# Attention and a SwiGLU block on one core: sums moved to VectorE, weight sums stored later into more places

## The chip, the cores and the metric

The kernel runs on one core of a Trainium2 chip. A core has five engines that each work through a list of instructions of their own, in order, and wait for each other by semaphores: TensorE (PE in the profile, its weight loads PEld), VectorE (DVE), ScalarE (ACT), GpSimd (POOL) and SyncE (SP), which here only issues transfers between the chip's memory (DRAM) and the core's memory (SBUF). Matrix products land in PSUM, eight banks of 128 x 512 floats. The metric is the time of the whole program on the device, in microseconds.

## The reference

```python
def _attn_ref(q, k, v, g_q, g_k):          # (8, 12, 448, 64) each: sequences, heads, tokens, width
    def rmsnorm(x, g):
        return x / np.sqrt(np.mean(x * x, axis=-1, keepdims=True) + 1e-06) * g
    q_n, k_n = rmsnorm(q, g_q), rmsnorm(k, g_k)
    scores = np.matmul(q_n, k_n.transpose(0, 1, 3, 2)) / np.sqrt(64)
    attn = softmax(scores)                 # written out in the original
    return np.matmul(attn, v)

def _moe_ref(x, w_gate, w_val, w_out, rms_g):   # x: (8 * 448, 768); weights 768 x 1536, 768 x 1536, 1536 x 768
    xn = x / np.sqrt(np.mean(x * x, axis=-1, keepdims=True) + 1e-06) * rms_g
    g = xn @ w_gate
    silu = g * (1.0 / (1.0 + np.exp(-g)))
    return silu * (xn @ w_val) @ w_out
```

The second function gets the first one's output, with the twelve heads side by side.

## The kernel before, in words

`safe_scores` does the work (a slower twin, `any_scores`, stands behind a flag and does not run here). Sequence by sequence and pair of heads by pair of heads it does attention; the block behind it (gate, value and out projections) of sequence b runs in the gaps of the attention of sequence b+1. The order is written out by hand. Each call of `pe` is one **step**: it raises a clock `now["t"]`, emits its work, and then emits what is due; `after(n, fn)` makes `fn` due n steps later. All five engines receive their instructions in the order in which they are emitted. `fill` takes the next entries of a list `todo` (each a product of the gate and value stage, or a part of the out projection) as steps; between them stand the steps of attention.

The first sequence (b = 0) multiplies directly, while the weights are converted from 64-bit floats. From the second on (b = 1 to 7), fewer products and more sums are used. For gate and value there are four **groups** of columns in the order 0, 2, 1, 3, and in each group fifteen products (`PRODUCTS`: q3, q6, q8, q9, q4, q5, q7, q2, q0, q1, q14, q11, q12, q10, q13), each of a left factor (a block of the normed attention output or a sum of such blocks) and a right factor. Right factors are nine blocks of weights (`RAWS`, b11 to b33) and nine sums of two or three of them (`RIGHT_G`, v1 to v14). `three` emits a group. It accumulates products one on top of another in PSUM banks called B, X, Y and Z, and takes **snapshots** in between: the bank's content after a product is copied or added into one of the six result tiles c11 to c23, or into the helpers s and d, before the next product is put on top of it. Three other products lie between two uses of a bank (two lie between a product's snapshot and the next writing). `copy` is a copy by ACT (L1177), `plus` adds PSUM to an SBUF tile on DVE (L1180), `more` adds two SBUF tiles on GpSimd (L1183). `hand` turns a finished pair of result tiles into the gated hidden values.

The nine sums of weights of each group are made once, during the second sequence, by `derive` (L1072, L1075, on DVE), stored to DRAM by SP (L1078, `after(1, ...)`), and loaded again for every later sequence. `ask` emits loads of weights (L1052) in a fixed order (`uses`) as places come free. **Places** are pieces of an SBUF tile `arena`: 66 units of 128 columns, a block of gate and value weights takes four neighbouring units, a block of out weights three. While the sums for the out projection are made, 18 units are set aside ("side"); 48 remain, 12 places of four. `ask` goes on only while `keep_free` more places are free than the one it takes: 2 for the second sequence's gate and value weights. A block's place is given back when its last use has been emitted, and counts as free one step later. `derive` takes the sum that is next on its list if its sources were asked for at least five steps ago; if a product is up whose sum has not been emitted, `fill` emits the sum right before it.

The out projection is built the same way, with seven right factors for each half: B11, B21, T2, T3, T1, B22, T4, where the T's are sums. `derive_o` makes those (L1102), in six columns c of four sums each, in the places set aside; the loads of any T wait until all 24 sums are stored. For b = 2, 3, 5, 6 and 7 the out projection goes a level deeper (`out_quads`, L1496; its sums of weights are made by `derive_q`, L1130 to L1133), for b = 1 and 4 it doesn't (`out_strassen`, L1425). Its left factors are sums of hidden values: `left_sums` (L1344) makes S1 to S4 for a pair of row tiles, `left_q1` (L1370) the deeper level's.

Two attention instructions matter beside this: `turn` transposes q and k on PE, and ACT (L549) and DVE (L550, L552) take the result; at a sequence's end `rms_x` (L725) sums the squares of its output, which GpSimd has added up in `ss` (L643).

Of the kernel before, what the change touches and what calls it, by code (L numbers as in the profile page):

```python
# [25 lines left out]
BW = 384  # L26
# [309 lines left out]
def safe_scores(  # L336
# [498 lines left out]
    freed = [0] * (NW * BW // 128)  # L835

    def h_of(fc):
        return hs[fc // KG][:, fc % KG, :]
# [10 lines left out]

    def places(kind):  # L850

        lim = len(freed) - (zone() if count["done"] else 0)
        if kind == "wg":
            spans = [range(i, i + 4) for i in range(0, lim - 3, 4)]
        elif kind == "side":
            spans = [range(i, i + 3) for i in range(lim, len(freed), 3)]
        else:
            spans = [range(i - 3, i) for i in range(lim, 2, -3)]
        return [span for span in spans if None not in [freed[i] for i in span]]

    def block(kind="w"):
        span = min(places(kind), key=lambda span: (max(freed[i] for i in span), span[0]))
        for i in span:
            freed[i] = None
        return arena[:, span[0] * 128:span[-1] * 128 + 128], span

    def room(many, kind="w"):
# [2 lines left out]
    def give_back(key):  # L870

        span = st.pop(key)[1]

        def free():
            for i in span:
                freed[i] = now["t"]

        after(1, free)

    def data(key):  # L880
        return st[key][0]
# [65 lines left out]
    def convert():  # L947

        n = turn_of["n"]
        if n >= TURNS or not room(1):  # L950
            return False
        turn_of["n"] += 1
        if 0 <= n - 5 < len(pieces):
            key = pieces[n - 5][0]
            st[key] = block()
            lo, top = st.pop(("cv", n - 5))
            nc.gpsimd.tensor_tensor(data(key).bitcast(I32), top, lo, ALU.add)
        if 0 <= n - 4 < len(pieces):
            st["cv", n - 4] = join(*st.pop(("cv", n - 4)))
        if 0 <= n - 3 < len(pieces):  # L960
            st["cv", n - 3] = split(st.pop(("raw", n - 3)), n - 3)
        if n < len(pieces):
            st["raw", n] = load_raw(pieces[n][1])
        if 0 <= n - 7 < len(pieces):
            keep(pieces[n - 7][0])
        if turn_of["n"] == TURNS:
            count["done"] = True
            ends = [cv_tile(i, F32) for i in range(6)]
            whole = [raw_pool.tile([128, 2 * BW], F32, name="raw") for _ in range(7)]
            room_so.extend(whole[:6])  # L970
            more_x.extend((ends[4], ends[5], whole[6][:, 0:S]))
            homes = [t[:, 0:BW] for t in ends[:4]]
            carried.extend(t.rearrange("p (c n) -> p c n", c=KG) for t in homes)
        return True
# [51 lines left out]
    def ask():  # L1026

        if turn_of["n"] < TURNS:
            return
        while side and room(1, "side"):  # L1030
            key = side.pop(0)
            asked[key] = now["t"]
            st[key] = block("side")
            nc.sync.dma_start(out=data(key), in_=home(key))
        while asked["n"] < len(uses):
            key = uses[asked["n"]]
            kind, keep_free = "wg" if key[0] == "wg" else "w", 3
            if key[1] == 1 and key[0] == "wg":
                keep_free = 2
            elif asked["derived"] < len(derived):  # L1040
                return
            if key[0] == "wo" and key[2][0] == "T" and asked.get("sums_o", 0) < 4 * NFP:
                return
            if key[0] == "wq" and asked.get("sums_q", 0) < KG * (key[2] + 1):
                return
            if not room(keep_free + 1, kind):
                return
            asked["n"] += 1
            asked[key] = now["t"]
            st[key] = block(kind)  # L1050
            src = home(key)
            nc.sync.dma_start(out=data(key)[:, 0:src.shape[-1]], in_=src)  # L1052

    def derive(wait=5):

        if asked["derived"] >= len(derived):
            return False
        g, to = derived[asked["derived"]]
        first, minus, plus = RIGHT_G[to]
        sources = [part.lstrip("-") for part in (first, minus, plus) if part]  # L1060
        for name in sources:
            if ("wg", 1, g, name) not in st or asked.get(("wg", 1, g, name), 0) > now["t"] - wait:
                return False
        if not room(1, "wg"):
            return False
        asked["derived"] += 1
        key = ("wg", 1, g, to)
        st[key] = block("wg")
        parts = {name: data(("wg", 1, g, name)) for name in sources}
        at, t = parts[first], data(key)  # L1070
        if minus:
            nc.vector.tensor_tensor(t, at, parts[minus], ALU.subtract)  # L1072
            at = t
        if plus:
            nc.vector.tensor_tensor(t, at, parts[plus.lstrip("-")], ALU.subtract if plus[0] == "-" else ALU.add)  # L1075
        for name in sources:
            done_with(("wg", 1, g, name))
        after(1, lambda: nc.sync.dma_start(out=home(key), in_=t))  # L1078
        return True

    def done_with(key):

# [4 lines left out]
    sums_o = [(c, step) for c in range(NFP) for step in (("T1", "B12", "B11", "B11"), ("T3", "B22", "B12", "B12"),  # L1087
                                                          ("T2", "B22", "T1", "B22"), ("T4", "B21", "T2", "B21"))]

    def derive_o(wait=5):  # L1090

        if not sums_o:
            return
        c, (to, plus, minus, place) = sums_o[0]
        for name in BLOCKS:
            if asked.get(("wd", 1, name, c), now["t"]) > now["t"] - wait:
                return
        sums_o.pop(0)
# [3 lines left out]
        nc.vector.tensor_tensor(data(key), a, b, ALU.subtract)  # L1102

        def store():
            keep(key)
            asked["sums_o"] = asked.get("sums_o", 0) + 1

        after(1, store)
        if to == "T4":
            for name in ("T1", "T2", "T3", "T4"):  # L1110
                after(3, lambda name=name: used(("wd", 1, name, c)))
# [55 lines left out]
    def three(b, n):  # L1167
# [11 lines left out]
        def plus(name, ps):  # L1179
            nc.vector.tensor_tensor(T[name], ps[:, 0:S], T[name], ALU.add)  # L1180

        def more(name, one, other, what):
            nc.gpsimd.tensor_tensor(T[name], T[one], T[other], what)  # L1183

        def hand(name, j, wait):

# [44 lines left out]
        def q5(make):  # L1231
            T["pc"] = pair("pc")
            T["c13"], T["c23"] = T["pc"][:, 0], T["pc"][:, 1]
            copy("c13", make(bank["Y"]))
            more("c13", "c13", "s", ALU.add)
            more("c13", "c13", "d", ALU.subtract)

        def q7(make):
            copy("c23", make(bank["B"]))
            more("d", "c23", "d", ALU.subtract)  # L1240

        def q2(make):
            copy("c11", make(bank["X"]))
            more("c11", "c11", "d", ALU.add)

        def q0(make):
            copy("c23", make(bank["Y"]))
            more("c23", "c23", "s", ALU.add)

        def q1(make):  # L1250
            plus("c21", make(bank["B"]))

        def q14(make):
            plus("c12", make(bank["X"]))
# [13 lines left out]
            plus("c13", ps)  # L1268

        def q13(make):  # L1270
            if n == len(GROUPS) - 1 and in_quads(b):
                after(1, lambda: left_q1(b, 0, range(3)))
            plus("c13", make(bank["Z"]))
            after(1, lambda: hand("pc", 2, 1))
            if n % 2:
                after(3, lambda: sums(0))
                after(3 if n == len(GROUPS) - 1 else 5, lambda: sums(1))

        def sums(i):

            st["left_sums"] = now["t"]
            if i < len(out_pairs(b)):
                left_sums(b, i, n // 2)

        def run(fn, left, right):
            fn(lambda onto=None: product(b, g, left, right, onto))
# [50 lines left out]
    def left_sums(b, n, half):  # L1337

        pair, row = (0, n) if in_quads(b) else (n, 0)
        if half == 0:  # L1340
            for i, name in enumerate(("S1", "S2", "S4")):
# [2 lines left out]
        ops = [lambda args=args: nc.vector.tensor_tensor(*(of(name) for name in args[:3]), args[3])  # L1344
               for args in (("S1", "A21", "A22", ALU.add), ("S2", "S1", "A11", ALU.subtract),
                            ("S3", "A11", "A21", ALU.subtract), ("S4", "A12", "S2", ALU.subtract))]
        if half and in_quads(b):
            first_sums.extend(ops)
        else:
# [255 lines left out]
    def fill(n=None):  # L1605
# [8 lines left out]
        for _ in range(min(n, len(todo))):  # L1614
# [266 lines left out]
```

## Time and profile before

| what | value |
|---|---|
| median of three runs | 1613.95 us (1613.63 to 1617.66) |
| profiled execution, device time | 1614.22 us |
| its span, first to last instruction | 1612.4 us |
| PE busy / DVE / ACT / POOL | 1508.5 / 981.7 / 639.6 / 898.2 us |
| moved by DMA | 322.5 MB, 200 GB/s on average |
| granted TensorE clock, mean | 0.98 |

Rows of the profile name the line, the engine, the operation and the tile written and read (`w<-w` is a weight place computed from other places, `kept` and `kept_o` the DRAM copies). "ff" is any PSUM bank of the block, "l" the tiles of s, d and some left factors, "pa", "pb" and "pc" the pairs c12/c22, c11/c21 and c13/c23, "raw", "top" and "xs" left factors in tiles used earlier for something else. A row of a wait gives the waiter, the one waited for, total us, the number of times, and the longest. A row of the order of time gives the start, the length, the instructions merged into it, and in square brackets the idle time before it and what ended it. One product of the gate and value stage is eight rows of PE (x8).

### The profile page before, as it was taken

Reading aid. Unit: us, or ns where it says so; the run is one execution under the profiler, and the core shown is the slowest. Engines: PE = TensorE matmul, PEld = TensorE weight load, DVE = VectorE, ACT = ScalarE, POOL = GpSimd, SP = SyncE. Lnnn points to the kernel's source line nnn. Section 1 sums busy time; section 2 is a strip of 40 time slices with the busy share of each in tenths; the row PEclk is TensorE's granted clock in tenths of the full one; section 3 lists DMA queues with packets and bytes.
Section 4 is the critical chain, followed back from the end, with each engine's and each line's share of the span. In section 5 each row is a group of like instructions: output and inputs, shape, how many; then the busy total and the mean of one; then the engine's idle time right before and its main releaser. Section 6 shows DMA issues by size and latency. Waiting matters only on the chain. (4 is left out here: it accounts for less than half of the span.)

```text
span 1612.4 us, 25793 instructions
## 1 busy us (share of the span) xinstructions
PE 1508.5 (94%) x8732; PEld 1170.4 (73%) x8732; DVE 981.7 (61%) x1766; ACT 639.6 (40%) x1409; POOL 898.2 (56%) x848
## 2 busy tenths in 40 slices
PE   8999989887788898899999999999999999999997
PEld 4344445676654687778887888857887888899997
DVE  5788897776664277685455844344546834484454
ACT  6766653433422243333543335524553244202210
POOL 6877976664442276445766566566655654413212
PEclk9999999999988999999999999999999999999999
DMA  7767674664447789987545874567545774578666
GB/s 209 206 187 212 195 219 153 210 211 140 145 144 228 236 280 298 291 257 247 168 133 157 260 233 142 162 188 217 158 131 178 228 221 119 146 241 280 170 207 194
DMA packets 302176, 322.51 MB, mean 200 GB/s; under 512 B 81620, under 2 KB 243668, under 8 KB 302036
## 3 DMA queue, kind: packets, MB, share of 16 engines
q1 hardware_dynamic: 301108, 320.58, 64.9%
q8 instruction: 72, 1.18, 0.3%
q14 instruction: 68, 0.56, 0.1%
q10 hardware_dynamic: 800, 0.20, 0.1%
q0 software_dynamic: 128, 0.00, 0.0%
HBM read 266.90 MB, written 53.77 MB: 199 GB/s over the span
## 5 line engine op out<-in xcount | busy, mean ns | idle before, releaser
L1162 PE MATMUL ff<-x,w 128*128 128x224 f32 x1344 | 278.6, 362 | 20.5 <-DVE w L1075 12.4
L1162 PEld LDWEIGHTS ff<-x,w 128*128 128x128 f32 x1344 | 258.1, 195 | 28.9 <-issue 10.2
L713 POOL TENSOR_TENSOR es<-es,e 128x448 f32<-128x448 f32 x205 | 244.5, 1193 | 12.2
L1183 POOL TENSOR_TENSOR pc<-pc,l 128x448 f32<-128x448 f32 x84 | 98.7, 1175 | 254.2 <-ACT pc L1177 231.2
L658 PE MATMUL sc<-qT,kT 64*64 64x448 f32 x1176 | 232.0, 539 | 4.4 <-DVE kT L552 2.1
L673 PE MATMUL av<-e,vt 64*64 64x448 f32 x984 | 193.6, 538 | 0.0
L1162 PE MATMUL ff<-xs,w 128*128 128x224 f32 x896 | 181.5, 358 | 8.8 <-DMA w<-kept 4.7
L1162 PEld LDWEIGHTS ff<-xs,w 128*128 128x128 f32 x896 | 170.6, 194 | 13.9 <-issue 7.7
L663 ACT ACTIVATE e<-sc 128x448 f32<-128x448 f32 x294 | 155.2, 546 | 61.3 <-PE sc L658 45.8
L1180 DVE TENSOR_TENSOR pb<-ff,pb 128x448 f32<-128x448 f32 x56 | 34.8, 621 | 189.7 <-PE ff L1162 187.0
L658 PEld LDWEIGHTS sc<-qT,kT 64*64 64x64 f32 x1176 | 78.9, 133 | 88.7 <-issue 59.1
L1496 PE MATMUL ff<-w,l 128*128 128x192 f32 x630 | 119.0, 330 | 14.7 <-issue 8.7
L1496 PEld LDWEIGHTS ff<-w,l 128*128 128x128 f32 x630 | 103.4, 190 | 22.0 <-issue 12.1
L515 POOL TENSOR_TENSOR rs<-ms,mhalf 128x12 f32<-128x12 f32 (+1 forms) x50 | 116.6, 2332 | 4.2
L708 POOL TENSOR_TENSOR es<-e 128x448 f32<-128x448 f32 x41 | 47.3, 1153 | 124.4 <-ACT e L663 124.4
L1564 PE MATMUL ff<-x,w 128*128 128x448 f32 x288 | 112.8, 545 | 0.0
L1162 PE MATMUL ff<-top_x,w 128*128 128x224 f32 x448 | 93.0, 357 | 3.1 <-DVE w L1075 2.0
L673 PEld LDWEIGHTS av<-e,vt 64*64 64x64 f32 x984 | 66.4, 133 | 39.3 <-issue 39.3
L1162 PEld LDWEIGHTS ff<-top_x,w 128*128 128x128 f32 x448 | 83.1, 190 | 15.2 <-issue 12.3
L1564 PEld LDWEIGHTS ff<-x,w 128*128 128x128 f32 x288 | 53.8, 192 | 51.6 <-issue 49.6
L550 DVE COPY kT<-tr 128x64 f32<-128x64 f32 x48 | 10.6, 220 | 130.9 <-ACT qT L549 130.8
L1162 PE MATMUL ff<-l,w 128*128 128x224 f32 x448 | 89.7, 353 | 0.0
(188 smaller groups left out, 2902.8 us busy)
## 6 DMA issues: line engine op xcount, KB each, us to landing
w<-kept SPq DMA_DIRECT2D x396, 256.0 KB, 3.7
w<-kept_q SPq DMA_DIRECT2D x350, 192.0 KB, 3.7
w<-kept_o SPq DMA_DIRECT2D x150, 192.0 KB, 3.8
kept_q<-w SPq DMA_DIRECT2D x63, 192.0 KB, 3.7
qk<-in_q_dram SPq DMA_DIRECT2D x48, 192.0 KB, 3.5
qk<-in_k_dram SPq DMA_DIRECT2D x96, 96.0 KB, 3.5
raw<-in_moe_w_gate_dram SPq DMA_DIRECT2D x24, 384.0 KB, 4.7
raw<-in_moe_w_val_dram SPq DMA_DIRECT2D x24, 384.0 KB, 4.1
```

The lines of the kernel that those rows point to most:

```text
L515: nc.gpsimd.tensor_tensor(st["rs", g][:, cols], ms, mhalf[:, cols], ALU.pow)
L550: nc.vector.tensor_copy(st["kT", g][:, LAST], ps[:, S:])
L658: nc.tensor.matmul(ps[r, 0:S], lhsT=st["kT", g][r, keys_of(i)], rhs=st["qT", g][r, :], start=True, stop=True)
L663: nc.scalar.activation(e, ps[:, 0:S], ACT.Exp)
L673: nc.tensor.matmul(st["av", g][own(j), 0:S], lhsT=vt, rhs=st["e", g, i][r], start=i == 0, stop=i == PARTS - 1, skip_group_check=True)
L708: nc.gpsimd.tensor_tensor(st["es", g], st["e", g, 0], st["e", g, 1], ALU.add)
L713: nc.gpsimd.tensor_tensor(st["es", g], st["es", g], st["e", g, i], ALU.add)
L1162: nc.tensor.matmul(bank[:, w * HT:(w + 1) * HT], lhsT=data(key)[:, (2 * w + c) * 128:(2 * w + c + 1) * 128], rhs=a[left][:, c, :], start=o ...
L1180: nc.vector.tensor_tensor(T[name], ps[:, 0:S], T[name], ALU.add)
L1183: nc.gpsimd.tensor_tensor(T[name], T[one], T[other], what)
L1496: nc.tensor.matmul(ps, lhsT=a[:, j, :], rhs=data(key)[:, n % 2 * HW:(n % 2 + 1) * HW], start=start and j == 0, stop=j == KG - 1, skip_grou ...
L1564: nc.tensor.matmul(bank[w][:, 0:S], lhsT=data(key)[:, c * 128:(c + 1) * 128], rhs=st["x", 0][:, 3 * half + c, :], start=half == c == 0, st ...
```

## The change

- In `three`, five steps of a group change their snapshots. `copy` followed by `more` on GpSimd becomes one sum from PSUM on DVE (`onto`, or `plus`): c13 = bank + s (q5), c23 = bank + s (q0), c11 = bank - d (q7) and then bank + c11 (q2). c13 minus d becomes a sum of two SBUF tiles on DVE. d keeps its value; the new c11 takes over what d was used for.
- `derive` stores a sum five steps after it is made, not one, and the sum's place is given back only when its product and its store have both been emitted. Places of the second sequence's gate and value weights count as free three steps after being given back, not one.
- Six more places for that sequence: the first 512 columns of the six tiles `room_so`, in which the left sums of out projections lie later. Loads must leave six places free instead of two.
- In `fill`, `derive` may emit up to two or three instructions' worth of sums a step instead of one sum, and is called in two more steps early in a block; `derive_o` is called up to three times. T blocks are asked for once their own sum's store is emitted, which happens two steps after the sum, and a sum needs its sources asked for four steps ago instead of five.
- Since `room_so` is taken until the end of the second sequence's products, that sequence's sixteen left sums come after its last group, one in each step, instead of eight in the middle and eight at the end.
- In sequences with the deeper out projection, the first three left factors (`left_q1(b, 0, range(3))`) are emitted at q1 of the last group, not one step after q13.

```diff
+    spare = {}
...
         if kind[0:2] == "wg":
             spans = [range(i, i + 4) for i in range(0, lim - 3, 4)]
+            if kind == "wg1":
+                spans += [range(i, i + 4) for i in sorted(spare) if i % 4 == 0]
...
-        after(1, free)
+        after(3 if key[0:2] == ("wg", 1) else 1, free)
...
+            for i, t in enumerate(room_so):
+                spare[1000 + 4 * i] = t[:, 0:4 * 128]
+                freed.update({1000 + 4 * i + j: 0 for j in range(4)})
...
             if key[1] == 1 and key[0] == "wg":
-                keep_free = 2
+                kind, keep_free = "wg1", 6
...
-            if key[0] == "wo" and key[2][0] == "T" and asked.get("sums_o", 0) < 4 * NFP:
+            if key[0] == "wo" and key[2][0] == "T" and ("kept", *key[2:]) not in asked:
                 return
...
-        after(1, lambda: nc.sync.dma_start(out=home(key), in_=t))
-        return True
+        def store():
+            nc.sync.dma_start(out=home(key), in_=t)
+            done_with(key)
+
+        after(5, store)
+        return len(sources) - 1
...
-    def derive_o(wait=5):
+    def derive_o(wait=4):
...
-            asked["sums_o"] = asked.get("sums_o", 0) + 1
-
-        after(1, store)
+            asked["kept", to, c] = True
+
+        after(2, store)
...
     def used(key):
         give_back(key)
-        after(1, ask)
+        after(3 if key[0:2] == ("wg", 1) else 1, ask)
...
-        def more(name, one, other, what):
-            nc.gpsimd.tensor_tensor(T[name], T[one], T[other], what)
+        def onto(name, ps, other, what=ALU.add):
+            nc.vector.tensor_tensor(T[name], ps[:, 0:S], T[other], what)
...
-            copy("c13", make(bank["Y"]))
-            more("c13", "c13", "s", ALU.add)
-            more("c13", "c13", "d", ALU.subtract)
+            onto("c13", make(bank["Y"]), "s")
+            nc.vector.tensor_tensor(T["c13"], T["c13"], T["d"], ALU.subtract)
 
         def q7(make):
-            copy("c23", make(bank["B"]))
-            more("d", "c23", "d", ALU.subtract)
+            onto("c11", make(bank["B"]), "d", ALU.subtract)
 
         def q2(make):
-            copy("c11", make(bank["X"]))
-            more("c11", "c11", "d", ALU.add)
+            plus("c11", make(bank["X"]))
 
         def q0(make):
-            copy("c23", make(bank["Y"]))
-            more("c23", "c23", "s", ALU.add)
+            onto("c23", make(bank["Y"]), "s")
 
         def q1(make):
             plus("c21", make(bank["B"]))
+            if n == len(GROUPS) - 1 and in_quads(b):
+                left_q1(b, 0, range(3))
...
         def q13(make):
-            if n == len(GROUPS) - 1 and in_quads(b):
-                after(1, lambda: left_q1(b, 0, range(3)))
             plus("c13", make(bank["Z"]))
...
-            if i < len(out_pairs(b)):
+            if b == 1:
+                if n == len(GROUPS) - 1 and i == 0:
+                    jobs = [left_sums(b, pair, half) for pair in range(2) for half in range(2)]
+                    first_sums.extend(fns[k] for ks in ((0, 1), (2,), (3,)) for fns in jobs for k in ks)
+            elif i < len(out_pairs(b)):
                 left_sums(b, i, n // 2)
...
+            if 2 < now["t"] - st["block"] < 5:
+                derive()
             if now["t"] - st["block"] > 4 and now["t"] != st.get("left_sums"):
-                if not derive():
+                made = 0
+                while made < 2:
+                    done = derive()
+                    if not done:
+                        break
+                    made += done
+                for _ in range(3 - made):
                     derive_o()
-                derive_o()
                 derive_q()
```

More of the change, by code (lines that the diff above doesn't have):

```diff
@@ L834, in safe_scores @@
     arena = slots.tile([128, NW * BW], F32, name="w")
-    freed = [0] * (NW * BW // 128)
+    UNITS = NW * BW // 128
+    freed = {i: 0 for i in range(UNITS)}
+    spare = {}
     def h_of(fc):
@@ L850, in places @@
     def places(kind):
-        lim = len(freed) - (zone() if count["done"] else 0)
-        if kind == "wg":
+        lim = UNITS - (zone() if count["done"] else 0)
+        if kind[0:2] == "wg":
             spans = [range(i, i + 4) for i in range(0, lim - 3, 4)]
+            if kind == "wg1":
+                spans += [range(i, i + 4) for i in sorted(spare) if i % 4 == 0]
         elif kind == "side":
-            spans = [range(i, i + 3) for i in range(lim, len(freed), 3)]
+            spans = [range(i, i + 3) for i in range(lim, UNITS, 3)]
         else:
@@ L864, in block @@
             freed[i] = None
+        if span[0] in spare:
+            return spare[span[0]], span
         return arena[:, span[0] * 128:span[-1] * 128 + 128], span
@@ L1063, in derive @@
                 return False
-        if not room(1, "wg"):
-            return False
+        if not room(1, "wg1"):
+            return 0
         asked["derived"] += 1
         key = ("wg", 1, g, to)
-        st[key] = block("wg")
+        st[key] = block("wg1")
+        refs[key] = 2
         parts = {name: data(("wg", 1, g, name)) for name in sources}
@@ L1281, in sums @@
             st["left_sums"] = now["t"]
-            if i < len(out_pairs(b)):
+            if b == 1:
[3 more added lines that the diff above has]
+            elif i < len(out_pairs(b)):
                 left_sums(b, i, n // 2)
         def run(fn, left, right):
-            fn(lambda onto=None: product(b, g, left, right, onto))
+            fn(lambda ps=None: product(b, g, left, right, ps))
         by_name = dict(q0=q0, q1=q1, q2=q2, q3=q3, q4=q4, q5=q5, q6=q6, q7=q7, q8=q8, q9=q9, q10=q10, q11=q11, q12=q12, q13=q13, q14=q14)
@@ L1346, in left_sums @@
                             ("S3", "A11", "A21", ALU.subtract), ("S4", "A12", "S2", ALU.subtract))]
+        if b == 1:
+            return ops
         if half and in_quads(b):
```

## The prediction

> **What bounds the kernel now.** I read the page's first two parts, then the busy time of each engine in a few stretches, then who waited for whom on PE, then the same on the DMA queue of SP, then the order of time around the long waits.
>
> ```profile
> span 1612.4 us, 25793 instructions
> PE 1508.5 (94%) x8732; PEld 1170.4 (73%) x8732; DVE 981.7 (61%) x1766; ACT 639.6 (40%) x1409; POOL 898.2 (56%) x848
> ```
>
> PE is the bound: it is idle for 1612.4 - 1508.5 = 103.9 us, and only that, with what a lowered clock costs, can be won. In the stretches below the columns are the length, then the busy time of PE, PEld, DVE, ACT and POOL, the granted clock, the DMA share and GB/s.
>
> ```profile
> 100.00:200.00 100.00, 97.91 (x456) 48.16 (x455) 85.29 (x138) 66.79 (x153) 85.80 (x80) 1.00 0.66 191
> ...
> 300.00:320.00 20.00, 16.62 (x111) 12.62 (x115) 19.43 (x25) 6.07 (x12) 13.68 (x11) 1.00 0.58 204
> ...
> 300.00:460.00 160.00, 130.57 (x739) 107.97 (x739) 119.70 (x178) 56.40 (x122) 91.00 (x79) 0.90 0.51 167
> 460.00:560.00 100.00, 86.05 (x398) 49.24 (x399) 37.53 (x78) 24.86 (x55) 25.63 (x25) 0.93 0.68 212
> ...
> 560.00:1612.00 1052.00, 1007.86 (x6234) 874.46 (x6232) 593.89 (x1110) 375.16 (x826) 553.82 (x515) 0.99 0.66 205
> ```
>
> The stretch 300 to 460 (gate and value products of the second sequence, whose weight sums are made on the chip) holds 29.4 us of PE's idle time at a clock of 0.90; the next (that sequence's out projection) 14 at 0.93; the last 1052 us hold 44 at 0.99. PE's waits (total us, times, longest):
>
> ```profile
> PE ff L1162 <- DVE w L1075: 26.2, 11, 6.7
> PE ff L1425 <- DMA w<-kept_o: 9.4, 3, 8.5
> PE ff L1496 <- issue: 8.7, 5, 2.0
> PE msx L725 <- POOL ss L643: 7.7, 5, 1.9
> PE ff L1162 <- DVE pb L1180: 7.5, 6, 1.5
> PE ff L1162 <- DMA w<-kept: 4.7, 1, 4.7
> PE ff L1162 <- DVE w L1072: 2.8, 2, 1.6
> ```
>
> PE stands 26.2 + 2.8 = 29.0 us for sums of weights. DVE is not full there (119.70 of 160), so the sums are late because their sources are. SP's queue between 300 and 460 says why:
>
> ```profile
> SPq L1078 <- DVE w L1075: 48.6, 24, 8.8
> SPq L1078 <- DVE w L1072: 12.3, 4, 4.8
> SPq L1052 <- DVE w L1072: 12.0, 3, 9.0
> ```
>
> L1078 stores a sum, L1052 loads weights. SP issues in order, so for 48.6 + 12.3 = 60.9 us it stands at stores whose sum DVE has not made, with the next loads behind; for 12.0 us it stands at loads into a place that a sum still reads. The waits also cost clock:
>
> ```profile
> 313.39 1.75 PE L1162 MATMUL ff<-x,w 128*128 128x224 f32 x8 [0.60 <-DVE w L1075]
> ...
> 330.65 3.35 PE L1162 MATMUL ff<-raw,w 128*128 128x224 f32 x8 [3.83 <-DVE w L1075]
> ...
> 372.20 3.36 PE L1162 MATMUL ff<-raw,w 128*128 128x224 f32 x8 [6.73 <-DVE w L1075]
> ...
> 406.59 7.37 PE L1162 MATMUL ff<-x,w 128*128 128x224 f32 x24 [4.12 <-DVE w L1075]
> ...
> 443.31 3.33 PE L1162 MATMUL ff<-x,w 128*128 128x224 f32 x8 [3.22 <-DVE w L1075]
> ...
> 491.58 10.77 PE L1425 MATMUL ff<-w,raw 128*128 128x384 f32 x24 [8.51 <-DMA w<-kept_o]
> ...
> 518.45 8.01 PE L1425 MATMUL ff<-w,raw 128*128 128x384 f32 x24
> ```
>
> After a wait of 0.60 us a product takes 1.75 us, after one of over 3 us 3.33 to 3.36: 1.6 us lost each time, 2.1 in the group of 24 (7.37 against three times 1.75), 2.8 at 491.58 against 518.45. These four losses in the stage make 6.9 us; a mean clock of 0.90 over 160 us bounds the loss at 16.
>
> **The change, part by part.**
>
> *Snapshots.* 28 groups of products (four for each of seven sequences). Rows of the copy, of the sum on GpSimd, of a sum from PSUM on VectorE, and of the sums of weights (ns: least, median, most):
>
> ```profile
> L1177 ACT COPY pc<-ff x84: 512/532/534, 307.9 to 1543.5; 128x448 f32<-128x448 f32 x84
> L1183 POOL TENSOR_TENSOR pc<-pc,l x84: 1125/1132/1594, 308.5 to 1544.3; 128x448 f32<-128x448 f32 x84
> L1180 DVE TENSOR_TENSOR pc<-ff,pc x84: 607/615/626, 326.9 to 1553.4; 128x448 f32<-128x448 f32 x84
> L1072 DVE TENSOR_TENSOR w<-w x28: 674/682/1622, 300.0 to 456.0; 128x512 f32<-128x512 f32 x28
> L1075 DVE TENSOR_TENSOR w<-w x32: 677/692/1542, 301.6 to 456.8; 128x512 f32<-128x512 f32 x32
> ```
>
> Each group loses four copies (112 x 0.532 = 60 us of ACT) and five sums on GpSimd (140 x 1.13 = 158 us of POOL); DVE gets four sums from PSUM and one (c13 minus d) between SBUF tiles: 140 x 0.62 = 87 us, making 1068 of 1612. The one between SBUF tiles I price at 0.62 too; it could be stretched as the sums of weights are (1622 against 682), by 0.9 us at most. In the second sequence's stage DVE gets 20 x 0.62 = 12.4 us. A removed sum on GpSimd also stretches DVE less. The two kinds of weight sums took 25.29 and 30.84 us in the stage, against 28 x 0.682 + 32 x 0.692 = 41.2 unstretched: 14.9 us of stretching.
>
> ```profile
> 300.00:460.00 160.00, 25.29 (x28) 0.90 0.51 167
> ...
> 300.00:460.00 160.00, 30.84 (x32) 0.90 0.51 167
> ```
>
> POOL ran 79 instructions there, 20 of them go, so by share 20/79 x 14.9 = 3.8 us of it goes. The Trainium skill, "SBUF — State Buffer", section "SBUF: two separate sides", has a stronger rule: a VectorE instruction with two SBUF inputs and a GpSimd instruction lock each other out for a whole instruction. By that rule up to 20 x 1.13 = 22.6 us of stretching could go, bounded by the 14.9 that there is; the sum of the stage would then be some 11 us lower. The row of the sums from PSUM (607 to 626 ns in all 84) agrees that these are not locked out.
>
> *Stores five steps later, places freed three steps later, six more places, two sums a step.* A step is one entry in the hand-made order; a product is one of 1.75 us. Five steps on, the sum has been made when SP meets its store, and the place after three steps no longer has a reader. Nothing is added to SP: the same 36 stores. What a later store costs is its place, held longer. Places were 12 (48 units of 4), and a load was asked for with 3 of them free; now there are 18 and 7 must be free: 11 instead of 9 can be taken when a load goes out, and seven stay for sums. Nothing reads a stored sum before the third sequence.
>
> The stage's new length: PE needs 130.57 - 6.9 (to 16) = 115 to 124 us. DVE needs 119.70 + 12.4 - 3.8, less eight left sums that move behind the stage (the first row below):
>
> ```profile
> 382.20 0.55 DVE L1344 TENSOR_TENSOR raw<-h,h 128x384 f32<-128x384 f32 x1
> ...
> 486.31 2.32 DVE L1102 TENSOR_TENSOR w<-w 128x384 f32<-128x384 f32 x4
> ...
> 682.48 0.56 DVE L1370 TENSOR_TENSOR l<-l,top 128x384 f32<-128x384 f32 x1
> ```
>
> 8 x 0.55 = 4.4, so DVE needs 123.9 us and is the tighter of the two. How full it can run: 97% in the slice from 300 to 320, 85% between 100 and 200 with PE at 98%. That makes 127.7 to 145.3 us; I take the middle, 137, since both are full stretches of this kernel: **23 us less** (15 to 32).
>
> *Sums for the out projection.* T2's loads were asked for only when all 24 sums were stored. The last four came at 486.31 and PE stood 8.51 us until 491.58. Now each load waits for its own sum, and up to three sums go into a step. Only the last of six has to come before PE reaches T2 at 483. Gain 8.5 + 2.8 (clock) = 11.3 at most, nothing at least if that last sum comes as late as now; I take **9**, near the upper end, since the sums gate loads in order. The sixteen left sums one at a time (8.8 us) lie where DVE is busy 37.53 of 100: nothing; without that cover 8.8 us. The wait of 4.7 for kept weights I leave as it is: it could go, or grow by as much.
>
> *First left factors in mid-group.* For five sequences PE waits "for nothing" (the row "issue": 8.7 us, 2.0 at most) at the second step of the out projection. With it, the rows for the next part:
>
> ```profile
> 683.14 1.21 PE L1496 MATMUL ff<-w,l 128*128 128x192 f32 x6 [1.66 <-issue]
> ...
> 666.78 1.25 POOL L1183 TENSOR_TENSOR pb<-pb,l 128x448 f32<-128x448 f32 x1
> 667.99 1.24 POOL L643 TENSOR_TENSOR ss<-ss,rd 128x448 f32<-128x448 f32 x1
> ...
> 669.29 0.95 PE L725 MATMUL msx<-ones,ss 128*112 128x1 f32 x8 [1.94 <-POOL ss L643]
> ```
>
> The second left sum (682.48, row above) ends at 683.04 and PE starts at 683.14: that is what it waits for. Emitted at q1, five products (8 us) earlier, the three sums (1.7 us) lie ahead of the last sums from PSUM instead. Of 8.7 us I take **7** (0 to 8.7). They push the next snapshot by 1.7 us, less than the two products (3.5 us) until its bank is written again.
>
> *GpSimd relieved.* ss follows a snapshot sum directly, and PE waits for it 1.9 us. Without the four sums of a group it comes over 1.94 us earlier. Of 7.7 us I take **6** (0 to 7.7).
>
> *Later groups.* For 24 groups the freeing of a PSUM bank passes from ACT to DVE's queue. Bounds: all of the 7.5 us of waits on pb L1180 go (ACT, which DVE's copies wait for, no longer stands behind GpSimd, last row below), or each group gains a wait as long as the longest in that row, 1.5 us: 36 more. I take **3 more**, near the lower end, because DVE mostly stands waiting for PE there (first row, after 560):
>
> ```profile
> DVE pb L1180 <- PE ff L1162: 170.6, 33, 14.0
> ...
> ACT pc L1177 <- POOL l L1183: 25.4, 13, 3.2
> ```
>
> Sum: -23 - 9 - 7 - 6 + 3 = **-42 us**. The profiled execution took 1614.22 us, 1.8 around its span; the median of the runs is 1613.95. So 1614.2 - 42 = **1572 us**.
>
> **Rivals.**
>
> *Places run out.* The sums keep theirs until stored, seven must be free for a load: the loads wait for places instead of for SP. For it: the places that loads may take grow from 9 to 11 only, and each is held at least two steps longer. Against it: SP's 72.9 us, which are waits for instructions, not for places. Then the stage and T2 stay as they are: -7 - 6 + 3 = -10, 1604 us.
>
> *DVE becomes the bound of the stage.* 123.9 us of work, and each snapshot that waits for its product holds the sums behind it. At 80% full the stage takes 155, so 5 less: -24 in all, 1590 us. Against it: the 85 and 97% above. "TensorE: Matmul & The Clock Gate" in the Trainium skill, section "Architectural detail", calls VectorE's queue strictly first in, first out, which is what such blocking needs; no row here shows VectorE overtaking.
>
> *Slower: banks wait for DVE.* After each turn of q and k DVE stands for ACT's qT, then reduces, and now also holds four banks' release. From (23 + 9 + 7 + 6) / 24 = 1.9 us a group on, the gain is eaten; at 2.4 us a group the time is 1614 - 45 + 58 = 1627. For it: the longest wait now is 1.5 us with less on DVE. Against it: three products lie between a bank's uses, and ACT is relieved.
>
> **How the numbers follow.** The forecast 0.60 (its own range 1552 to 1587: below, the 9 us to the stage's end, 6 to the upper ends of the next three terms and 5 of the clock; above, the 8 us to the stage's other end and 7 in the later groups), DVE bound 0.15, places 0.13, slower 0.12. A measurement of this kernel can tell about 0.3%, 5 us, from no change. The places' case reaches into that band with 0.05. So faster 0.82, same 0.06, slower 0.12. The range 1552 to 1606 leaves out the slower case, part of the places' case and a little below.
>
> **What would show it.** PE's waits on L1075 and L1072 under 10 us, the clock in that stage above 0.96, SP's waits at its stores under 15 us; no wait of 8 us for kept_o; PE's "issue" waits and msx gone; L1180's waits by PE under 15 us. It is wrong if those last grow past 40 us, or if the sums' waits stay near 29 while SP's go: then places or DVE's order, not SP, held the sums back.

## The result, and the profile after

The changed kernel takes **1555.2 us** (median; 1554.9 to 1558.9), the kernel before 1614.9 in the same series: a ratio of 0.9633, 95% interval 0.9613 to 0.9653, so 60 us or 3.7% less. Forecast were 1572 and 1552 to 1606. The profiled execution took 1555.48 us (before: 1614.22), its span is 1553.7. From the page:

```profile
span 1553.7 us, 25676 instructions
PE 1493.5 (96%) x8732; PEld 1163.8 (75%) x8732; DVE 1051.9 (68%) x1906; ACT 582.2 (37%) x1297; POOL 732.1 (47%) x708
```

PE is idle for 60.2 us instead of 103.9, and the same 8732 matmuls are busy for 15.0 us less, at a mean granted clock of 0.99 instead of 0.98. ACT lost 57 us, POOL 166, DVE gained 70.

Three stages cut at the same matmuls show where the time came from: from the second sequence's first gate product to its end (764 rows of PE in both), from there to the first attention inside the third sequence's products, and the rest (6260 rows in both). First before, then after:

```profile
294.10:459.30 165.20, 135.11 (x764) 112.34 (x763) 121.19 (x181) 60.56 (x134) 93.91 (x82) 0.91 0.51 168
459.30:555.50 96.20, 82.11 (x379) 45.08 (x377) 38.16 (x78) 22.82 (x51) 25.63 (x25) 0.93 0.68 212
555.50:1612.40 1056.90, 1012.36 (x6260) 878.95 (x6256) 593.92 (x1110) 377.19 (x830) 553.82 (x515) 0.99 0.66 205
```

```profile
296.80:437.50 140.70, 125.50 (x764) 104.85 (x763) 119.30 (x193) 52.20 (x118) 68.90 (x62) 0.98 0.61 202
437.50:518.00 80.50, 76.97 (x381) 42.70 (x378) 43.10 (x84) 22.82 (x51) 27.25 (x26) 1.00 0.75 234
518.00:1553.70 1035.70, 1008.82 (x6260) 879.79 (x6256) 662.02 (x1232) 328.02 (x734) 411.75 (x395) 0.99 0.67 209
```

The first stage lost 24.5 us (forecast 23), the second 15.7 (forecast 9), the rest 21.2 (forecast 10). Ahead of them 2.7 us were lost, in a part whose code hardly differs: of the kernels below, u_place, u_both, u_snap and k2 reach the same place at some 294 us, as early as the kernel before. In the first two stages the columns also show the clock: PE's busy time fell by 9.6 and 5.1 us for the same work.

PE's waits after:

```profile
PE tr L544 <- DVE kT L550: 14.2, 5, 5.1
PE ff L1177 <- DMA w<-kept: 4.9, 3, 3.5
...
PE ff L1177 <- DVE raw L1085: 2.5, 2, 1.3
...
PE ff L1177 <- DVE w L1085: 1.1, 1, 1.1
...
PE msx L725 <- POOL ss L643: 0.7, 1, 0.7
```

The 29.0 us for sums of weights are down to 4.3 (raw and w on L1085, and 0.7 on L1082, not shown); the waits for kept_o, "issue" and nearly all of ss are gone. New on top is kT (L550), 14.2 us instead of 5.7. SP's queue during the second sequence's products, however, was a surprise:

```profile
SPq L951 <- DVE w L1117: 40.5, 12, 8.4
SPq L951 <- DVE kT L550: 11.7, 1, 11.7
...
SPq L1090 <- DVE raw L1082: 3.7, 1, 3.7
SPq L1090 <- DVE raw L1085: 3.6, 3, 2.8
```

SP no longer stands at the stores of gate and value sums (L1090), but it stands 52 us at stores of sums for the out projection (L951). It is hardly freer than before, and the stage is 24.5 us shorter all the same.

### The profile page after: what moved, and what is told of

Same layout as the page of the kernel before. It is cut to its first block, busy times and chain, and to the rows that moved or that the text cites. A ratio compares the mean times of both kernels' runs of the same rounds, so it can differ in the third digit from the quotient of the medians.

```text
span 1553.7 us, 25676 instructions
## 1 busy us (share of the span) xinstructions
PE 1493.5 (96%) x8732; PEld 1163.8 (75%) x8732; DVE 1051.9 (68%) x1906; ACT 582.2 (37%) x1297; POOL 732.1 (47%) x708
## 5 line engine op out<-in xcount | busy, mean ns | idle before, releaser
L1177 PE MATMUL ff<-x,w 128*128 128x224 f32 x1272 | 259.9, 359 | 0.9 <-DVE pb L1198 0.5
L713 POOL TENSOR_TENSOR es<-es,e 128x448 f32<-128x448 f32 x205 | 251.2, 1225 | 13.6
L1177 PEld LDWEIGHTS ff<-x,w 128*128 128x128 f32 x1272 | 243.5, 194 | 5.0 <-issue 1.4
L1177 PE MATMUL ff<-xs,w 128*128 128x224 f32 x848 | 168.9, 353 | 6.6 <-DMA w<-kept 4.9
L1177 PEld LDWEIGHTS ff<-xs,w 128*128 128x128 f32 x848 | 158.5, 190 | 10.8 <-issue 8.6
L643 POOL TENSOR_TENSOR ss<-ss,rd 128x448 f32<-128x448 f32 x40 | 46.7, 1169 | 209.3 <-ACT rd L642 208.0
L1198 DVE TENSOR_TENSOR pc<-ff,l 128x448 f32<-128x448 f32 x56 | 34.9, 623 | 122.3 <-PE ff L1177 75.3
L1195 DVE TENSOR_TENSOR pb<-ff,pb 128x448 f32<-128x448 f32 x84 | 52.3, 623 | 66.2 <-PE ff L1177 58.8
L1581 PEld LDWEIGHTS ff<-x,w 128*128 128x128 f32 x288 | 54.5, 194 | 52.6 <-issue 50.6
L1177 PE MATMUL ff<-top_x,w 128*128 128x224 f32 x424 | 88.0, 357 | 2.4 <-ACT pa L1192 1.2
L1177 PEld LDWEIGHTS ff<-top_x,w 128*128 128x128 f32 x424 | 78.6, 190 | 14.2 <-issue 10.5
```

The costliest lines, as they stand in the source:

```text
L643: after(m, lambda: (nc.gpsimd.tensor_tensor(ss, ss, rd, ALU.add), st.update({("summed", b): hp})))
L713: nc.gpsimd.tensor_tensor(st["es", g], st["es", g], st["e", g, i], ALU.add)
L1177: nc.tensor.matmul(bank[:, w * HT:(w + 1) * HT], lhsT=data(key)[:, (2 * w + c) * 128:(2 * w + c + 1) * 128], rhs=a[left][:, c, :], start=o ...
L1198: nc.vector.tensor_tensor(T[name], ps[:, 0:S], T[other], what)
L1581: nc.tensor.matmul(bank[w][:, 0:S], lhsT=data(key)[:, c * 128:(c + 1) * 128], rhs=st["x", 0][:, 3 * half + c, :], start=half == c == 0, st ...
```

## The experiments

**Store early again (u_store).** Theory: SP's queue; rival: places and the order of the sums.

```diff
-        after(5, store)
+        after(1, store)
-        after(3 if key[0:2] == ("wg", 1) else 1, free)      # and the same for ask
+        after(1, free)
```

> The changed kernel with each sum stored one step after it is made, and places free again after one step; the six places and the order of the sums stay. Theory (SP stood at the stores and held the loads back): the second sequence's stage goes back to about 160 us, 1573 us in all, with SP waiting some 60 us at stores of sums. Rival (the places and the two sums a step did it): 1557 us, with SP waiting all the same.

1558.8 us (1555.3 to 1560.7). SP stood 57.6 us at L1090, and the stage took 144.1 us.

```profile
SPq L1090 <- DVE w L1085: 36.4, 21, 5.6
SPq L1090 <- DVE raw L1085: 12.3, 7, 3.0
SPq L1090 <- DVE raw L1082: 4.5, 1, 4.5
SPq L1090 <- DVE w L1082: 4.4, 2, 3.7
```

```profile
296.30:440.40 144.10, 127.56 (x765) 106.43 (x764) 115.68 (x193) 52.13 (x118) 67.68 (x62) 0.95 0.64 212
```

The theory falls: SP's waits are back and the stage stays 21 us shorter than before.

**Take the six places away (u_place).**

```diff
-                kind, keep_free = "wg1", 6
+                keep_free = 2
# derive takes its place with kind "wg" again
```

> The changed kernel without the six more places (two are left free again instead of six); stores stay late. Theory (SP's queue was what mattered): a little is lost because late stores hold places longer, 1560 us. Rival (places were what was short): the stage goes back by 15 us or more, 1570 us or above, PE waiting for sums of weights.

1642.1 us (1641.6 to 1642.4), slower than the kernel before: ratio to it 1.0167 (1.0150 to 1.0184). The stage, 764 rows of PE, and PE's largest wait in it:

```profile
294.30:521.40 227.10, 156.56 (x764) 125.18 (x763) 123.52 (x210) 52.08 (x118) 67.15 (x62) 0.82 0.46 146
```

```profile
PE ff L1177 <- DVE w L1085: 68.5, 25, 5.1
```

227 us, with a clock of 0.82, DVE at 54%. DVE waited for no load in this stage, so the sums stood late in its order: with only 12 places, sums held until their store leave none for the next load or the next sum. Which of these two runs short first the trace does not tell, since places are counted in the written order. That is the rival "places run out" of the prediction, seen without the six more.

**Both undone (u_both)**: the edits of u_store and u_place together.

> The changed kernel without the six places and with sums stored and places freed after one step, as before; the snapshots, the faster making of sums and the rest stay. Since SP stood 58 us at stores in the kernel with early stores and that cost 3 us, while late stores in 12 places cost 87, theory: places held too long and too few were the bound, late stores made the need worse, so with early stores in 12 places the stage is about as before the change (165 us), 1580 us in all. Rival (late stores hurt only because six places were missing, and without either the order of the sums alone brings the gain): 1560 us.

1558.3 us (1555.0 to 1564.6), the stage 145.3 us, though SP stood 51 us at these stores and there were 12 places. The rival was right.

```profile
294.40:439.70 145.30, 127.75 (x764) 105.70 (x763) 123.85 (x202) 52.21 (x118) 70.87 (x62) 0.97 0.65 210
```

```profile
SPq L1090 <- DVE w L1085: 45.6, 21, 7.1
...
SPq L1090 <- DVE w L1082: 5.0, 2, 2.5
```

So with sums emitted up to two a step, late stores and more places cancel. With early stores places are also freed after one step, with late ones after three; loads leave two of the 12 places free, or six of the 18. The four combinations give

| | 12 places | 18 places |
|---|---|---|
| stores after one step | 1558.3 us, stage 145.3 | 1558.8, stage 144.1 |
| stores after five steps | 1642.1, stage 227.1 | 1555.2, stage 140.7 |

The 3 us between 1555.2 and the other two good ones lie inside their overlapping ranges.

**Places alone, on the kernel before (o_place)**: the spare places, `keep_free` of 6, and the left sums of that sequence after its last group; stores after one step and at most one sum a step as before.

```diff
+                spans += [range(i, i + 4) for i in sorted(spare) if i % 4 == 0]
...
-                keep_free = 2
+                kind, keep_free = "wg1", 6
...
```

> The kernel before with the six more places alone (six left free by loads), and the second sequence's left sums after its last group, since they share the tiles. Theory (places were short): the stage falls from 165 to about 150 us, 1598 us, though SP still stands at stores. Rival (only with late stores and two sums a step): 1612 us.

1592.9 us (1591.7 to 1598.9), ratio 0.9856 (0.9826 to 0.9886). The stage took 141.7 us, as short as with the whole change (in the slowest of its four runs, 1598.9), and SP stood at the stores as before:

```profile
296.90:438.60 141.70, 127.06 (x765) 105.77 (x764) 119.70 (x173) 60.78 (x134) 92.82 (x80) 0.96 0.63 205
```

```profile
SPq L1088 <- DVE w L1085: 38.5, 22, 5.5
SPq L1088 <- DVE raw L1082: 10.9, 1, 10.9
SPq L1088 <- DVE raw L1085: 7.2, 5, 4.1
```

Either cure is enough: more places (with six left free by loads), or what u_both keeps of the change, more sums a step above all; the snapshots alone leave the stage as it was (o_snap below). Both kernels also have that sequence's left sums behind its last group, which no run undid by itself. That move can't be the whole cause: in the kernel before, 14.7 of the 29.0 us that PE waits for sums lie ahead of the first left sum at 382.20, and in o_place 4.1 us of such waits are left in the whole stage.

What both cures change is how early a sum stands in DVE's order: the last of these sums ends 1.7 us ahead of the stage's end in the kernel before, 10.0 in o_place and 4.8 in u_both. In the kernel before, DVE waited for no load of weights in the whole stage; its one wait for a transfer at a sum was for a place that a store still read (first row). Ahead of PE's longest wait, until 372.20, the sum came last behind 5.4 us of DVE's other work:

```profile
DVE w L1072 <- DMA kept<-w: 1.3, 1, 1.3
```

```profile
365.38 0.23 DVE L550 COPY kT<-tr 128x64 f32<-128x64 f32 x1 [1.12 <-ACT qT L549]
...
369.22 1.14 DVE L1180 TENSOR_TENSOR pc<-ff,pc 128x448 f32<-128x448 f32 x2
...
370.75 0.68 DVE L1072 TENSOR_TENSOR w<-w 128x512 f32<-128x512 f32 x1
371.46 0.69 DVE L1075 TENSOR_TENSOR w<-w 128x512 f32<-128x512 f32 x1
```

The sources had landed when DVE came to the sum; the sum stood late in its order. `derive` counts steps of the written order, not time, so a wait of SP while the program runs can't move a sum in that order. Which condition in the kernel before kept it late (a place, a source not yet asked for, or one sum a step) was not separated further.

**Fewer places left free (k2)**: 18 places, loads leave two free.

```diff
-                kind, keep_free = "wg1", 6
+                kind, keep_free = "wg1", 2
```

> The changed kernel with 18 places but only two of them left free by loads, instead of six. Theory (what counts is that a sum finds a place at once): loads take the places and sums wait again, 1565 us or more. Rival (the number of places alone counts, and earlier loads help): 1550 to 1556 us.

1572.6 us (1571.2 to 1573.4); the stage took 159.8 us.

```profile
PE ff L1177 <- DVE w L1085: 19.1, 6, 4.5
```

The theory held, in the time and in this wait: with late stores it counts that loads leave places for sums.

**Sums for the out projection as before (u_sumso).**

```diff
-            if key[0] == "wo" and key[2][0] == "T" and ("kept", *key[2:]) not in asked:
+            if key[0] == "wo" and key[2][0] == "T" and asked.get("sums_o", 0) < 4 * NFP:
# derive_o(wait=5), store after one step, one or two calls a step
```

> The changed kernel with the sums for the out projection as before: one or two a step, T's loads only when all 24 sums are stored. Theory: the wait of 8 us for T2 and its clock come back, 1566 us. Rival (the sums are early enough since the stage runs better): 1556 us, no such wait.

1568.1 us (1566.5 to 1573.3), 13 more. The wait for T2 is back, with the slow group behind it:

```profile
469.74 10.64 PE L1442 MATMUL ff<-w,raw 128*128 128x384 f32 x24 [8.56 <-DMA w<-kept_o]
```

**Snapshots as before (u_snap).**

```diff
-            onto("c13", make(bank["Y"]), "s")
-            nc.vector.tensor_tensor(T["c13"], T["c13"], T["d"], ALU.subtract)
+            copy("c13", make(bank["Y"]))
+            more("c13", "c13", "s", ALU.add)
+            more("c13", "c13", "d", ALU.subtract)
# q7, q2 and q0 likewise
```

> The changed kernel with the five snapshots of a group as before (copies by ACT, sums on GpSimd). Theory: in the last 1036 us the snapshots brought some 14 of the 21 us gained (ACT no longer stands behind GpSimd, ss comes earlier), and in the second sequence's stage they cost DVE time that it had: 1569 us, with PE waiting for ss and for pb again. Rival: the snapshots cost DVE time in the second sequence's stage, and the rest gained from the left factors alone: 1550 us.

1585.2 us (1584.8 to 1588.8): 30 us more, twice what I had left for it. The stage took 147.6 us, 7 more, and begins 2.2 us earlier; 24.6 more lie behind it. There PE waits for ss and pb:

```profile
PE msx L725 <- POOL ss L643: 8.7, 4, 2.3
PE ff L1177 <- DVE pb L1195: 8.1, 6, 1.6
```

**Snapshots alone, on the kernel before (o_snap)**: the same edit the other way.

> The kernel before with the change of snapshots alone. Theory: the last 1050 us become some 14 us shorter (ss and pb no longer waited for), the second sequence's stage gets a few us longer because DVE has 12 us more work there: 1603 us. Rival (the snapshots only pay where DVE's sums are early): 1614 us or more, PE waiting for banks in the second sequence.

1592.7 us (1591.9 to 1594.7), ratio 0.9864 (0.9844 to 0.9884): the part alone is worth 22 us, twice what I expected, with a stage of 164.7 us, unchanged. All of it comes later. The stretch from the second sequence's last gate product to the end, before and with the snapshots alone:

```profile
459.30:1612.40 1153.10, 1094.47 (x6635) 924.03 (x6633) 632.08 (x1188) 400.02 (x881) 579.45 (x540) 0.99 0.67 205
```

```profile
461.20:1591.70 1130.50, 1086.05 (x6635) 920.72 (x6633) 698.51 (x1309) 351.51 (x785) 436.69 (x420) 0.99 0.69 209
```

Idle time fell by 14.2 us (mostly by the waits for ss, 7.1, and pb, 6.7) and busy time, for the same 6635 rows, by 8.4. Cut into stretches of 20 us, the kernel before had three behind 560 us, apart from the very end, with a clock of 0.91 to 0.93; with the snapshots on DVE there is none. The first of the three contains the wait of 1.94 us for ss:

```profile
660.00:680.00 20.00, 17.45 (x92) 16.60 (x91) 12.06 (x21) 6.12 (x15) 19.36 (x18) 0.91 0.86 274
```

**A tile of its own for q7's copy (b_tile)**: ACT freed from GpSimd without moving any work.

```diff
-            copy("c23", make(bank["B"]))
-            more("d", "c23", "d", ALU.subtract)
+            T["own"] = tmp.tile([128, S], F32, name="th", tag="th", bufs=2)
+            copy("own", make(bank["B"]))
+            more("d", "own", "d", ALU.subtract)
```

> The kernel before with one edit: q7's copy goes to a tile of its own, not to c23, so ACT's later copy to c23 need not wait for GpSimd to read it; GpSimd and DVE have the same work as before. Theory (PE waited for pb because ACT stood behind GpSimd, and DVE behind ACT): PE's waits of 10 us on L1180 after 560 us mostly go, those for ss stay: 1606 us. Rival (they came from DVE's own load or GpSimd's): 1614 us, the waits unchanged.

1610.7 us (1609.4 to 1613.3), ratio 0.9973 (0.9963 to 0.9982). The 29.1 us that ACT stood behind GpSimd are gone, and PE's wait for pb halves:

```profile
PE ff L1162 <- DVE pb L1180: 3.6, 2, 2.6
```

That is some 4 of the 22 us. The chain ACT behind GpSimd, DVE behind ACT, PE behind DVE is real but small.

**ss on DVE (b_ss)**: the sum of squares leaves GpSimd's queue, on the kernel before.

```diff
-            after(m, lambda: (nc.gpsimd.tensor_tensor(ss, ss, rd, ALU.add), ...
+            after(m, lambda: ((nc.vector if b else nc.gpsimd).tensor_tensor(ss, ss, rd, ALU.add), ...
```

> The kernel before with one edit: from the second sequence on the sum of squares (ss) is added by DVE, not by GpSimd. DVE gets 35 x 0.6 us. Theory: PE's waits of 7.1 us for ss in four places go and nothing else does, 1608 us. Rival (a late ss also delays what follows, and GpSimd's other work gets earlier): 1600 us.

1604.1 us (1602.3 to 1605.4), ratio 0.9927 (0.9904 to 0.9950): 11 us, midway between the two. The same 6635 rows:

```profile
460.00:1602.30 1142.30, 1091.28 (x6635) 922.56 (x6633) 647.32 (x1213) 401.15 (x881) 555.73 (x515) 0.99 0.68 207
```

Idle time falls by 7.6 us, of which 7.1 are the wait for ss, and busy time by 3.2. So the four waits of 1.7 to 1.9 us cost about half as much again as they measure, but not each alike. In the kernel before, the same wait of 1.71 us, with the eight one-column products of msx behind it, is followed once by 24 rows at the usual length and once by 24 slow ones:

```profile
1050.10 0.95 PE L725 MATMUL msx<-ones,ss 128*112 128x1 f32 x8 [1.71 <-POOL ss L643]
...
1051.27 4.71 PE L1162 MATMUL ff<-x,w 128*128 128x224 f32 x24
...
1215.62 0.95 PE L725 MATMUL msx<-ones,ss 128*112 128x1 f32 x8 [1.71 <-POOL ss L643]
...
1216.79 6.39 PE L1162 MATMUL ff<-x,w 128*128 128x224 f32 x24
```

Of the four, two were followed by 24 rows of 6.39 us and two by 24 rows of 4.71. With ss on DVE three of these groups take 4.71 us; the first takes 6.03, behind a wait of 2.09 us for kT.

**First left factors after q13 again (u_q1).**

```diff
         def q13(make):
+            if n == len(GROUPS) - 1 and in_quads(b):
+                after(1, lambda: left_q1(b, 0, range(3)))
# and none of it in q1
```

> The changed kernel with the first three left factors one step after q13, as before. Theory: five waits of 1.7 us come back, 1563 us. Rival (with the snapshots on DVE the queue in front of them is longer at q13, so more comes back): 1570 us.

1558.3 us (1554.6 to 1561.6): not to be told from 1555.2 (1554.9 to 1558.9). The waits for "issue" are back, but those for kT after 530 us fell from 5.7 to 1.3:

```profile
PE ff L1513 <- issue: 6.0, 4, 1.8
...
PE tr L544 <- DVE kT L550: 1.3, 1, 1.3
```

DVE's order of time in the changed kernel, at q1 of a last group, and PE's row behind it:

```profile
622.22 0.62 DVE L1195 TENSOR_TENSOR pb<-ff,pb 128x448 f32<-128x448 f32 x1 [0.89 <-PE ff L1177]
622.76 0.55 DVE L1387 TENSOR_TENSOR l<-h,h 128x384 f32<-128x384 f32 x1
623.34 1.37 DVE L1387 TENSOR_TENSOR l<-l,top 128x384 f32<-128x384 f32 x1
624.64 1.48 DVE L1387 TENSOR_TENSOR h<-top,h 128x384 f32<-128x384 f32 x1
...
627.24 0.22 DVE L550 COPY kT<-tr 128x64 f32<-128x64 f32 x1
...
627.51 0.55 PE L544 MATMUL tr<-ident,qk 128*128 128x128 f32 x3 [2.68 <-DVE kT L550]
627.89 6.39 PE L1177 MATMUL ff<-x,w 128*128 128x224 f32 x24
```

The three sums, 3.40 us together, and four short sums of weights behind them (1.2 us, the rows left out) now stand ahead of the copy that frees the bank for k's turn: PE waits 2.68 us there, and the next 24 rows take 6.39 us, where 4.71 is usual. The other two waits of this kind, 1.48 and 1.49 us, are followed by 24 rows of 6.39 us too. What the left factors win at the out projection is given back here.

**kT's short copy on ACT (n_kt)**, on the changed kernel: this wait taken away.

```diff
-            nc.vector.tensor_copy(st["kT", g][:, LAST], ps[:, S:])
+            nc.scalar.copy(st["kT", g][:, LAST], ps[:, S:])
```

> The changed kernel with one more edit: the short copy of k's last 64 columns (L550) by ACT, right after its own qT, not by DVE. PE waits 14.2 us in five places for that copy (5.1 in the first sequence, 3.5 in the second). Theory: DVE's queue delays it and ACT has just read the same bank, so most of the 14 us goes: 1544 us. Rival: ACT's queue is as late, or the wait moves to the next work of DVE: 1555 us.

**1546.8 us** (1545.4 to 1548.1), ratio to the kernel before 0.9576 (0.9556 to 0.9595), the best of all: 8 us under the changed kernel. No wait for L550 is left; part of it moved, since at 260 us scores now wait 6.4 us for DVE's scaling of x:

```profile
PE sc L658 <- DVE x L743: 7.0, 2, 6.4
```

## Why the prediction was right or wrong

The direction, the stages and the range were right; the size was short by 17 us (-42 forecast, -59 between the profiled executions). Point by point:

- *The second sequence's stage, -23:* measured -24.5, and DVE ran at 119.30 of 140.70, 85%, the lower of the two fullnesses I had set bounds by. The step that failed is the one under it, "the sums are late because their sources are. SP's queue ... says why". SP stood as long at stores in u_store, u_both and o_place, with stages of 142 to 145 us. A long wait in a queue was taken for a cause without showing that anything needed sooner stood behind it; DVE itself waited for no load there. What held the sums was their place in DVE's order, which more places or more sums a step moved forward. That the stage came out 1.5 us from the forecast with this step wrong is luck in part: 137 us was the middle between two fullnesses, whatever kept the sums. The late store, priced as the cure, gave nothing that can be measured, and with 12 places costs 84 us.
- *Places:* they gave the gain on the kernel before (o_place, 23.5 us in the stage, with the left sums moved), and the rest of the change gave nearly the same without them (u_both, 19.9). The prediction priced neither by itself.
- *Sums for the out projection, -9:* the stage gave 15.7. The mechanism held (u_sumso costs 13 us). Of the 15.7, 10.6 are idle time (9.4 of kept_o and 1.2 of the wait for kept weights behind) and 5.1 PE's busy time, where I had counted 2.8 for the clock; the 2.3 us kept back for T2 loads still late did not come.
- *First left factors, -7:* the waits went (8.7 to 0 in the profile), but u_q1 shows no difference that can be told. I had priced the three sums at 1.7 us, and in the group shown they took 3.40; and I had checked their delay against PSUM banks and not against kT's copy in the same queue.
- *GpSimd relieved, -6, and later groups, +3:* together -3, against -22 for the snapshots alone. The wait for ss fell by 7.0 us, near the forecast, but with the busy time that goes with it it is worth 11 (b_ss). In the later groups the sign was wrong: waits on pb, pa and pc fell from 10.0 us to 1.2; b_tile shows 4 us of it as ACT's stand behind GpSimd. If the parts add up, the rest of the 22 us, some 7, was not separated.
- *The slower rival:* no sign of it. Its mechanism, work in front of DVE's queue, came through at another place, kT's copy: 5.7 to 14.2 us.
- *What would show it:* waits for sums under 10 us, the clock above 0.96 and no kept_o wait came true. SP's waits at the stores of gate and value sums fell to 7.3 us, but 52 us at stores of sums for the out projection took their place; in u_store, where 57.6 us of the first kind are back, the time is the same to 4 us.

## What to carry to other kernels

A queue that waits long is no cause until something needed sooner is shown behind it: undo the wait alone and look. Holding a buffer until its store is out needs more buffers: without them it was worse than the early store here (1642 against 1558 us), while the added buffers did no harm with the early store. When work moves to an engine, look for the short instruction in that engine's order that frees a bank for the bound engine; moving that one alone gave 8 us here.

## What the runs showed of the hardware

A wait of PE can cost clock as well as time even when it is short of 3 us, and its length alone does not decide it. After 2.68 us, together with eight one-column products before it, 24 rows took 6.39 us instead of 4.71; after 1.71 us in the kernel before they took 6.39 in one place and 4.71 in two others. Removing 7.6 us of idle time (b_ss) also took 3.2 us from the busy time of the same matmuls. The Trainium skill, "TensorE: Matmul & The Clock Gate", section "HAM oscillation", puts the bound at idle gaps of about 3.4 us. The waits of 3.83 and 6.73 us of the kernel before agree; that of 3.22 us, with a product of 3.33 us behind it, and those of 2.68 and 1.71 us lie below it. Whether one-column products count as idle, and what decides between two equal waits, no run here separates.

The sums from PSUM on DVE took 607 to 626 ns in every one of 308 cases after the change, while sums of weights between SBUF tiles reached 1.56 us (0.69 at the median). The Trainium skill, "SBUF — State Buffer", section "SBUF: two separate sides", counts VectorE's instructions with two SBUF inputs among those that contend with a GpSimd instruction which reads SBUF. The rows agree: of these two kinds of sums only the second is stretched.
